# Attention, router and experts on one core: routing weights stored beside the gathered rows, a smaller index table, and a new order of loads and router work

## The chip, the core and the metric

The kernel runs on one core of a Trainium2 chip. The metric is the device time of one execution in microseconds (us), as the median of several runs. Six names recur. PE is the matrix engine (its weight loads, PEld, run beside it), DVE the vector engine, ACT the scalar engine, POOL the GpSimd engine, SP the engine that here only issues DMAs. Each engine works through its own instructions in order and waits for the others by semaphores; DMAs run on 16 DMA engines shared by all queues.

## The reference

Two stages. The first is causal attention with a window of 64 positions, for 8 batches, 8 heads, 576 positions, 64 elements a head. Its output is written as 4608 rows of 512 floats. The second sends each row to one of 8 experts:

```python
logits = x @ w_gate                       # 4608 x 8
local_gate = sigmoid(x @ w_local)
for b in range(B):
    prev_e = -1
    for s in range(S):
        fresh_e = argmax(logits[b, s])
        e = fresh_e if s == 0 or local_gate[b, s] < 0.5 else prev_e
        prev_e = e
        p = softmax(logits[b, s])
        out[b, s] = p[e] * (relu(x[b, s] @ w1[e]) @ w2[e])
```

The expert of a row is therefore carried along the sequence until a gate lets a fresh choice in. w1[e] is 512 x 1024, w2[e] is 1024 x 512, all float32.

## The kernel before

**Attention.** There are 36 units of work: 9 stretches of 512 rows (`sc`, 0 to 8), each with 4 pairs of heads (`hp`). For a unit (sc, hp), `scores` puts a product of q and k into PSUM and ACT takes the exponential (L414). Then the window's mask is applied in one of two ways. For most units DVE multiplies by a mask (L419, 128x1024). For the units listed in `BIASED` PE adds a large negative bias in bfloat16 ahead of the exponential, six more matmuls, and DVE has nothing to do. `values` multiplies by v on PE (L429) into a pair of PSUM banks, of which there are two; DVE takes the reciprocal of the row sums (L434), for sc of 4 and more the gate columns (L437), and writes x (L439), which frees the pair. Scores are two units ahead (`LEAD`). At a stretch's last unit x goes to `xs` in device memory by a DMA on POOL. `xs` holds 4608 rows of 512 floats and two rows of zeros.

**Router.** It runs twice, as a generator whose steps are laid between other work: `first` for the first T1 = 1728 rows (14 chunks of 128) while attention still runs, `second` for the other rows (23 chunks) while the first expert blocks run. `gate` finds the fresh expert and the carried one (`vk`, transposed on PE at L806; `loc` and `carry` at L816 and L826; `ex` at L838; one-hots `oh`, summed on PE) and the probability `pt` of the chosen expert. `places` gives each row a place: a slot `hi` and a row `lo` within it. `table` turns places into lists of row numbers: for each chunk, a one-hot of `lo` (`rowh`, 128 x 128, L939) times a one-hot of `hi` multiplied by five columns (`colh`, L949): the chunk number, the position in the chunk, and the probability split into three bfloat16 parts. These products are summed on PE in PSUM (L956), copied to `t` (L958) and combined to the row number `idx`, the gather list `gx`, and the probability `pw` of each slot. Ahead of the expert blocks that use the second table, a flag is transposed (L159) and read.

**Experts.** A block is a group of 256 rows (or 128, 64, 32) of one expert. Block n takes its rows with gathers on POOL (L1133, 128 rows each, in `rows`), its weights with two loads of 2 MB on SP (L1148, in `weights`, from a ring of four buffers), transposes the rows (`turn`, L1162), then `hidden` and `result`. The last multiplies by `pw` as it empties PSUM: on ACT (L1393), or on DVE (L1274), and POOL scatters y to the output. Blocks -1, -2 and -3 come from the first table, and run in a plain or half-plain way (L1356, L1388) while `second` proceeds between their matmuls; blocks from 0 on come from the second table. Most of these use a scheme with 7 products in place of 8 (L1217, L1265).

**Order.** In attention the order of PE's instructions follows a scheduler. In `run`, PE's order is that of the program (`manual_schedule`), and from block -3 on that of DVE and ACT too; SP's is not. The router's steps are laid by `step`: it is called between groups of expert matmuls, counts down a `pause` by 3.5 per call, and takes up the next router steps when `pause` is used up; each step adds its own estimated length to `pause` with `yield`. The gathers of -1 and the loads of its w1 are issued from attention, at unit (7, 1), w2 at (8, 0), each behind a small DMA (`late`) that waits for a value of that unit; blocks -2 and -3 are fetched in `run`. Gathered rows live in six buffers (`xq`; -1 has two of its own in `xp`).

Of the kernel before, what the change touches and what calls it, by code (L numbers as in the profile page):

```python
# [8 lines left out]
F32 = mybir.dt.float32  # L9
# [25 lines left out]
PIECE = 10  # L35
T1 = 3 * S
# [31 lines left out]
BIASED = [(4, 3), (5, 1), (5, 3), (6, 1), (6, 3)]  # L68
# [13 lines left out]
def kernel(  # L82
# [21 lines left out]
    xs = dram.tile([N + 2, D], F32, name="xs")  # L104
    lt = const.tile([P, C, E + 1], F32, name="lt")
    tabs = dict(idx=const.tile([P, NS], U32, name="idx"), pw=const.tile([P, NS], F32, name="pw"),
                ej=const.tile([1, NBLK + 1], I32, name="ej"), idxh=const.tile([P, E], U32, name="idxh"),
                pwh=const.tile([P, E], F32, name="pwh"),
                idxq=const.tile([P, E], U32, name="idxq"), pwq=const.tile([P, E], F32, name="pwq"), idx1=const.tile([P, FIRST], U32, name="idx1"),
                pw1=const.tile([P, FIRST], F32, name="pw1"), ej1=const.tile([1, FB], I32, name="ej1"),  # L110
# [11 lines left out]
    with ExitStack() as fast:  # L122
        ring = fast.enter_context(tc.tile_pool(name="ring", bufs=4))
        rt = Router(fast, tc, lt, tabs, ident)
        ex = Experts(fast, tc, ring, *moe)
        zrow = ex.xp.tile([P, D], F32, name="xg")[:1]
        nc.vector.memset(zrow, 0.0)
        for i in (ZR, N + 1):
            nc.gpsimd.dma_start(out=xs[i:i + 1, :], in_=zrow)
        attention(tc, ring, kq, v3, v4, vt, vh, xs, lt, ok, wgs, wg2s, ident, rt, ex)  # L130
        ex.run(fast, rt, lambda ps: flag(nc, ps, ok, bad, tabs["ej"][:, NBLK:], rare, ident))
    if_rare = nc.values_load(rare[0:1, 0:1], min_val=0, max_val=1,  # L132
                             skip_runtime_bounds_check_because="the larger of two comparisons")
    with tc.If(if_rare > 0):
        if_bad = nc.values_load(bad[0:1, 0:1], min_val=0, max_val=1,
                                skip_runtime_bounds_check_because="the result of a comparison")
        with tc.If(if_bad > 0):
            careful(tc, q, k, v, xs, lt, wgs, ident)
            with ExitStack() as slow:
                ring = slow.enter_context(tc.tile_pool(name="ring2", bufs=4))  # L140
                rt = Router(slow, tc, lt, tabs, ident)
                rt.prepare()
                ex = Experts(slow, tc, ring, *moe)
                with tc.tile_pool(name="rt_ps1", bufs=1, space=PSUM) as ps:
                    for _ in rt.first(lambda: ps.tile([P, SC], F32, name="a")):
                        pass
                ex.begin()
                ex.run(slow, rt)
# [17 lines left out]
def attention(ctx, tc, ring, kq, v3, v4, vt, vh, xs, lt, ok, wg, wg2, ident, rt, ex):  # L166
# [302 lines left out]
    for i, (sc, hp) in enumerate(units):  # L469
# [50 lines left out]
        if (sc, hp) == (NSC - 2, 1):  # L520
# [4 lines left out]
        if (sc, hp) == (NSC - 1, 0):  # L525
            ex.weights(ex.jobs[0], -1, ("w2",), lambda: until(3, allr[:1, sc, hp, 0, :1]))
        if hp == HP - 1:
# [3 lines left out]
            nc.gpsimd.dma_start(out=xs[row_of(sc * SC):row_of(sc * SC) + SC, :].rearrange("(c p) d -> p c d", p=P),  # L531
# [12 lines left out]
def careful(ctx, tc, q, k, v, xs, lt, wgs, ident):  # L544
# [107 lines left out]
    def rows(st):  # L652
# [7 lines left out]
        nc.gpsimd.dma_start(out=xs[row_of(c * P):row_of(c * P) + P, :], in_=x)  # L660
# [36 lines left out]
class Router:  # L697
# [9 lines left out]
    def __init__(self, ctx, tc, lt, tabs, ident):  # L707
        self.nc, self.lt, self.tabs, self.ident = tc.nc, lt, tabs, ident
# [7 lines left out]
    def prepare(self):  # L716
# [24 lines left out]
        self.w = tl("w", P, CV, 5, dt=BF16)  # L741
        for i, a in enumerate((0, C1)):
            c = PART[i]
            n = c.stop - c.start
            nc.vector.tensor_copy(self.w[:, a:a + n, 0], iota(f"chunk{i}", [P, n], [[1, n]], 0, c.start - C))
        nc.vector.tensor_copy(self.w[:, :, 1], iota("at", [P, CV], [[0, CV]], 1))
# [21 lines left out]
    def gate(self, part, psum):  # L768
# [109 lines left out]
        vec.tensor_tensor(pt, pt, sm, op=Alu.mult)  # L878

        w = self.w[:, cs]  # L880
        vec.tensor_copy(w[:, :, 2], pt)
        vec.tensor_tensor(pt, pt, w[:, :, 2], op=Alu.subtract)
        vec.tensor_copy(w[:, :, 3], pt)
        vec.tensor_tensor(w[:, :, 4], pt, w[:, :, 3], op=Alu.subtract)
# [43 lines left out]
    def table(self, psum, cs, ns, lo, hi, idx, pw, gx):  # L928
# [5 lines left out]
        for k in range(0, len(pieces), 2):  # L934
            built = []
            for b, m in pieces[k:k + 2]:
                rowh = self.oh_p.tile([P, PIECE, P], BF16, name="rowh")[:, :m]
                sh = [P, m, P]
                vec.tensor_tensor(rowh, self.io128.to_broadcast(sh), last(lo[:, b:b + m]).to_broadcast(sh),  # L939
                                  op=Alu.is_equal)  # L940
                yield 0.15 * m, False
                one = self.oh_p.tile([P, PIECE, 1, ns], BF16, name="one")[:, :m]
                sh = [P, m, ns]
                vec.tensor_tensor(one[:, :, 0], self.ios[:, :, :ns].to_broadcast(sh),
                                  last(hi[:, b:b + m]).to_broadcast(sh), op=Alu.is_equal)
                colh = self.oh_p.tile([P, PIECE, 5, ns], BF16, name="colh")[:, :m]
                sh = [P, m, 5, ns]
                w = self.w[:, cs.start + b:cs.start + b + m, :].rearrange("p c (k o) -> p c k o", o=1)
                vec.tensor_tensor(colh, one.to_broadcast(sh), w.to_broadcast(sh), op=Alu.mult)  # L949
                built.append((b, m, rowh, colh))  # L950
                yield 0.3 + 0.0055 * ns * m, (b, m) in (pieces[-1], pieces[k + 1:k + 2] and pieces[k + 1])
            if tab is None:
                tab = psum()[:, :5 * ns].rearrange("p (k s) -> p k s", k=5)
# [3 lines left out]
        t = self.tl("t", P, 5, NS)[:, :, :ns]  # L957
# [10 lines left out]
        vec.tensor_tensor(pw, t[:, 2], t[:, 3], op=Alu.add)  # L968
        vec.tensor_tensor(pw, pw, t[:, 4], op=Alu.add)
        return at  # L970

    def first(self, psum):
# [29 lines left out]
        yield from self.table(psum, slice(0, C1), FIRST, lo, hi, tabs["idx1"], tabs["pw1"], tabs["gx1"])  # L1002

    def second(self, psum):
# [81 lines left out]
        at = yield from self.table(psum, slice(0, CV), NS, lo, hi, tabs["idx"], tabs["pw"], tabs["gx"])  # L1086

        for i in range(2):
            vec.tensor_scalar(tabs["idxh"][i * HF:(i + 1) * HF], at[:HF, HF0:], 2.0, float(i), Alu.mult, Alu.add)
            vec.tensor_copy(tabs["pwh"][i * HF:(i + 1) * HF], tabs["pw"][:HF, HF0:])  # L1090
        a = slice(HF, HF + QR)
        for i in range(4):
            vec.tensor_scalar(tabs["idxq"][i * QR:(i + 1) * QR], at[a, HF0:], 4.0, float(i), Alu.mult, Alu.add)
            vec.tensor_copy(tabs["pwq"][i * QR:(i + 1) * QR], tabs["pw"][a, HF0:])
# [8 lines left out]
class Experts:  # L1103
# [12 lines left out]
    def rows(self, st, n):  # L1116
        tabs = self.tabs
        if n < 0:
            idx, pw, gx, rows = tabs["idx1"], tabs["pw1"], tabs["gx1"], ZR + 1
            slots = range(-2 - 2 * n, -2 * n)  # L1120
        else:
            idx, pw, gx, rows = tabs["idx"], tabs["pw"], tabs["gx"], N + 2
# [3 lines left out]
        st.update(x=[], slots=slots, idx=idx, pw=pw, rows=P, big=len(slots) == 2, fast=len(slots) == 2 and n not in PLAIN)  # L1126
# [4 lines left out]
        for s in slots:  # L1131
            x = (self.xp if n == -1 else self.xq).tile([P, D], F32, name="xg")
# [3 lines left out]
            st["x"].append(x)  # L1136
        return st
# [17 lines left out]
    def turn(self, st, quiet, later=False):  # L1155
# [3 lines left out]
        for i, x in enumerate(st["x"]):  # L1159
# [3 lines left out]
            (nc.scalar.copy if quiet else nc.vector.tensor_copy)(xt[:, :, i * P:i * P + n], tp[:, :, :n])  # L1163
        if st["fast"] and not quiet and not later:
# [84 lines left out]
    def big_result(self, st, hooks):  # L1249
# [10 lines left out]
        pw = [st["pw"][:, i:i + 1] for i in st["slots"]]  # L1260
# [38 lines left out]
    def quarter(self, st):  # L1299
# [20 lines left out]
        def two():  # L1320
# [7 lines left out]
            nc.scalar.activation(y, yp, Act.Copy, scale=self.tabs["pwq"][:, s:s + 1])  # L1328
# [36 lines left out]
    def result(self, st, step, hooks=()):  # L1365
# [3 lines left out]
        if "half" in st:  # L1369
# [8 lines left out]
            nc.scalar.activation(y[:, :w], yp[:, :w], Act.Copy, scale=self.tabs["pwh"][:, s:s + 1])  # L1378
# [6 lines left out]
        for i, s in enumerate(st["slots"]):  # L1385
# [7 lines left out]
            nc.scalar.activation(y, yp, Act.Copy, scale=st["pw"][:, s:s + 1])  # L1393
# [13 lines left out]
    def run(self, ctx, rt, last=None):  # L1407
# [4 lines left out]
        ctx.enter_context(tc.manual_schedule(engines={ET.PE}))  # L1412
# [33 lines left out]
        jobs += [self.fetch(n) for n in order[1:FB]]  # L1446
        self.turn(jobs[0], True)
        step()
        for i, n in enumerate(order):
            quiet = i < FB  # L1450
            if i == FB - 1:
# [5 lines left out]
                ctx.enter_context(tc.manual_schedule(engines={ET.PE, ET.DVE, ET.Activation}))  # L1457
# [82 lines left out]
```

## Time and profile before

| what | us |
|---|---|
| time, median of 3 runs (lowest to highest) | 653.27 (651.92 to 654.65) |
| the profiled execution's own time | 650.66 |
| its span in the profile | 648.9 |
| mean granted PE clock | 0.995 of full |
| HBM read and written | 145.85 and 19.27 MB |

The page cuts the span into 40 equal slices of 16.2 us. A digit is the busy share in tenths, 9 standing for 90% and more:

```profile
DVE  6786588954996767346371775172826663876730
ACT  3766755621111231203130223012121321123120
POOL 4422121320014110131211311021213111200001
PEclk9999998999999999999999999999999999999998
DMA  9989999796437556486966855587768655945601
```

The seven first slices are attention, with DMA nearly full. From the eighth on the expert blocks of the first table begin, with the second part of the router beside them on DVE (slices 11 to 12 show DVE full). From about the thirteenth on the blocks of the second table run to the end.

The costliest groups of the page are the experts' matmuls (L1217, L1265, L1356, L1388), 227 us of PE's 621 in their three largest rows (79.6, 77.6 and 65.9, with a fourth of 56.2 and more behind). In attention the mask is DVE's largest group: 31 multiplies of 1296 ns in the mean, 40.1 us. DMAs of 2 MB of weights take 9.1 us from issue to landing in the median, gathers of 128 rows 8.0, the scatters of y 8.1.

### The profile page before, as it was taken

How to read it: one execution, taken by the hardware profiler on the slowest of the kernel's cores; microseconds unless marked ns; L12 is line 12 of the kernel's file. 1: busy time of each engine (PE TensorE's matmuls, PEld its weight loads, DVE VectorE, ACT ScalarE, POOL GpSimd, SP SyncE). 2: the span in 40 equal slices, each digit the busy share in tenths (PEclk: the TensorE clock that was granted, in tenths of full speed). 3: DMA queues.
4: the chain of work that ended last, by engine and by line, in shares of the span. 5: the costliest groups of instructions: out<-in, count | busy, mean ns of one | idle time of the engine just before them, and what ended most of it. 6: DMA issues, size and time to landing. Idle time of an engine off the chain costs nothing. (4 is left out here: it accounts for less than half of the span.)

```text
span 648.9 us, 14685 instructions
## 1 busy us (share of the span) xinstructions
PE 620.9 (96%) x6307; PEld 535.3 (82%) x6307; DVE 402.5 (62%) x737; ACT 184.6 (28%) x323; POOL 128.7 (20%) x131
## 2 busy tenths in 40 slices
PE   8898987998999999999999999999999999999995
PEld 7777775775757999979899799978997998899994
DVE  6786588954996767346371775172826663876730
ACT  3766755621111231203130223012121321123120
POOL 4422121320014110131211311021213111200001
PEclk9999998999999999999999999999999999999998
DMA  9989999796437556486966855587768655945601
GB/s 339 410 338 376 377 369 336 267 417 261 163 144 234 190 205 250 163 289 226 388 246 225 309 185 212 220 323 287 302 212 304 246 189 181 389 166 190 236 17 39
DMA packets 22003, 165.78 MB, mean 255 GB/s; under 512 B 3457, under 2 KB 4487, under 8 KB 11944
## 3 DMA queue, kind: packets, MB, share of 16 engines
q1 hardware_dynamic: 13112, 135.24, 56.6%
q0 software_dynamic: 8816, 29.50, 11.7%
q8 instruction: 52, 0.85, 0.5%
q14 instruction: 23, 0.19, 0.1%
HBM read 145.85 MB, written 19.27 MB: 254 GB/s over the span
## 5 line engine op out<-in xcount | busy, mean ns | idle before, releaser
L1338 POOL DMA_INDIRECT out_dram<-y,idx x36 | 41.8, 1162 | 313.7 <-DVE y L1274 127.1
L1217 PE MATMUL hp<-xs,ws 128*128 128x128 f32 x672 | 79.6, 275 | 0.0
L1265 PE MATMUL hp<-ws,hs 128*128 128x256 f32 x336 | 77.6, 380 | 0.0
L1217 PEld LDWEIGHTS hp<-xs,ws 128*128 128x128 f32 x672 | 77.3, 192 | 0.0
L1265 PEld LDWEIGHTS hp<-ws,hs 128*128 128x128 f32 x336 | 63.5, 190 | 9.3 <-issue 0.8
L1356 PE MATMUL hp<-xt,w 128*64 128x64 f32 (+2 forms) x640 | 65.9, 275 | 0.0
L1274 DVE SCALAR_TENSOR_TENSOR y<-hp,pw,kept 128x256 f32<-128x256 f32 x42 | 19.7, 481 | 73.1 <-issue 44.1
L1356 PEld LDWEIGHTS hp<-xt,w 128*128 128x128 f32 (+1 forms) x640 | 60.8, 170 | 4.6 <-issue 1.1
L1133 POOL DMA_INDIRECT xg<-xs,gx x40 | 46.7, 1168 | 82.1 <-PE tp L1162 68.5
L1228 DVE TENSOR_TENSOR h<-hp,keep 128x512 f32<-128x512 f32 x42 | 28.7, 690 | 52.7 <-PE hp L1217 52.0
L1388 PE MATMUL yp<-w,h 128*128 128x512 f32 x128 | 56.2, 592 | 0.0
L1217 PEld LDWEIGHTS hp<-xt,w 128*128 128x128 f32 x448 | 53.2, 192 | 2.7 <-issue 1.3
L1217 PE MATMUL hp<-xt,w 128*128 128x128 f32 x448 | 54.7, 275 | 0.0
L1265 PE MATMUL hp<-w,h 128*128 128x256 f32 x224 | 53.6, 382 | 0.0
L429 PE MATMUL xo<-vb,p 128*64 128x74 f32 (+1 forms) x576 | 44.3, 229 | 8.9 <-DVE x L439 4.0
L419 DVE TENSOR_TENSOR p<-p,mask 128x1024 f32<-128x1024 f32 x31 | 40.1, 1296 | 16.5 <-ACT p L414 16.3
L429 PEld LDWEIGHTS xo<-vb,p 128*64 128x64 f32 x576 | 38.7, 138 | 13.8 <-issue 6.3
L414 ACT ACTIVATE p<-sp 128x512 f32<-128x512 f32 x72 | 39.1, 596 | 33.2 <-PE sp L383 31.1
L383 PEld LDWEIGHTS sp<-w 64*64 64x64 f32 x1296 | 37.5, 136 | 11.9 <-issue 8.4
L1265 PEld LDWEIGHTS hp<-w,h 128*128 128x128 f32 x224 | 41.3, 190 | 5.6 <-issue 0.4
L1388 PEld LDWEIGHTS yp<-w,h 128*128 128x128 f32 x128 | 23.7, 190 | 26.8 <-issue 25.8
L383 PE MATMUL sp<-w 64*64 64x128 f32 (+1 forms) x1296 | 42.7, 267 | 1.7 <-ACT p L414 1.1
(284 smaller groups left out, 955.4 us busy)
## 6 DMA issues: line engine op xcount, KB each, us to landing
w<-in_w_dram SPq DMA_DIRECT2D x48, 2048.0 KB, 9.1
w<-in_kq_dram SPq DMA_DIRECT2D x17, 1024.0 KB, 9.8
xs<-x POOLq DMA_DIRECT2D x9, 1024.0 KB, 12.2
va<-in_v_dram SPq DMA_DIRECT2D x5, 1184.0 KB
vtt<-in_vt_dram SPq DMA_DIRECT2D x5, 1024.0 KB, 5.9
va<-in_v_dram SPq DMA_DIRECT2D x3, 1040.0 KB, 9.2
va<-in_v_dram SPq DMA_DIRECT2D x2, 520.0 KB, 8.0
w<-in_kq_dram SPq DMA_DIRECT2D x2, 512.0 KB, 3.8
```

The lines of the kernel that those rows point to most:

```text
L383: nc.tensor.matmul(sp[j][c * WIN:(c + 1) * WIN, a:b], lhsT=kt[h, hp, block * WIN:(block + 1) * WIN], rhs=qt[h, hp, a:b], start=not biased, ...
L414: nc.scalar.activation(p[:, j], sp[j], Act.Exp, scale=DH ** -0.5)
L419: masked.append(nc.vector.tensor_tensor(p, p, m.to_broadcast([P, 2, SC]), op=Alu.mult))
L429: nc.tensor.matmul(xo[par * WIN:(par + 1) * WIN, j, s * VW:s * VW + n], lhsT=p[:, j, b * WIN:(b + 1) * WIN], rhs=w[:, s, 2 * hp + j, :n], ...
L1133: self.nc.gpsimd.indirect_dma_start(out=x, out_offset=None, in_=self.xs[:rows, :], in_offset=bass.IndirectOffsetOnAxis(ap=gx[:, s:s + 1], ...
L1217: nc.tensor.matmul(out[:, m, :], lhsT=a[:, kk, m * P:(m + 1) * P], rhs=b[:, kk, :], start=start and m + kk == 0, stop=stop and (m, kk) == ...
L1228: nc.vector.tensor_tensor(o, x, y, op=add)
L1265: nc.tensor.matmul(out, lhsT=a[:, m, :], rhs=b[:, m, :], start=start and m == 0, stop=stop and m == FK // 2 - 1, skip_group_check=True)
L1274: nc.vector.scalar_tensor_tensor(y[i][:, j * w:(j + 1) * w], x, pw[i], y2, Alu.mult, Alu.add)
L1338: self.nc.gpsimd.indirect_dma_start(out=self.out[:, :], out_offset=bass.IndirectOffsetOnAxis(ap=st["idx"][:, s:s + 1], axis=0), in_=y, in_ ...
L1356: nc.tensor.matmul(hp[a, i, :], lhsT=st["w1"][:, kk, m * P:(m + 1) * P][:, a], rhs=st["xt"][:, kk, :n], start=(kk == 0), stop=(kk == DK - 1))
L1388: nc.tensor.matmul(yp, lhsT=st["h"][:, m, i * P:(i + 1) * P], rhs=st["w2"][:, m, :], start=(m == 0), stop=(m == FK - 1))
```

## The change

- Rows of `xs` become 528 floats wide (`PITCH`). The 16 added floats hold the row's probability. `weigh` writes them from SP, with a run of 64 bytes for each row: part 0 in two DMAs for 1728 rows, part 1 in three for 2880; the added floats of a few rows between the parts are zeroed at the start from POOL. A gathered tile then has its probabilities in a column, and `result` uses that column (`st["pw"]`) in place of the table's; halves and quarters copy it to a tile of their own.
- The table has two columns (chunk and position) in place of five, made by two DVE operations of 54 columns a chunk. The matmuls of the second table are 108 wide instead of 270, those of the first 12 instead of 30. The five small operations that split the probability, and those that put it together, go.
- The second table's row one-hots are made on ACT: for each of 37 slices of 128 x 128 the absolute value of `lo` less a ramp, then four times (10 slices at a time, or what is left) one less that, cut at zero. The first table's stay on DVE.
- In `run`, SP follows the order of the program too. The gathers of -2 and -3 are issued first, and a small DMA (`held`) on SP waits for the second gather of -2 before the weights of -2 and -3 are issued.
- The gates of the loads of -1 move two units ahead: w1 from (7, 1) to (6, 3), w2 from (8, 0) to (7, 1).
- Units (6, 0) and (6, 2) become biased.
- After the first `step` in `run` the pause is 2.0 longer. In PE's order the transposes of `vk` then come behind 32 matmuls of `hidden(-1)` and not 16, and the later router steps move back likewise.

```diff
-BIASED = [(4, 3), (5, 1), (5, 3), (6, 1), (6, 3)]
+BIASED = [(4, 3), (5, 1), (5, 3), (6, 0), (6, 1), (6, 2), (6, 3)]
...
-    xs = dram.tile([N + 2, D], F32, name="xs")
+    xs = dram.tile([N + 2, PITCH], F32, name="xs")
...
+        nc.gpsimd.dma_start(out=xs[T1:ZR, D:].rearrange("(c p) o -> p c o", p=HF),
+                            in_=zeros[:HF, :n * (PITCH - D)].rearrange("p (c o) -> p c o", c=n))
...
-        if (sc, hp) == (NSC - 2, 1):
+        if (sc, hp) == (NSC - 3, 3):
             ex.jobs = [ex.weights({}, -1, ("w1",), lambda: until(2, allr[:1, sc, hp, 0, :1]))]
...
-        if (sc, hp) == (NSC - 1, 0):
+        if (sc, hp) == (NSC - 2, 1):
             ex.weights(ex.jobs[0], -1, ("w2",), lambda: until(3, allr[:1, sc, hp, 0, :1]))
...
-        vec.tensor_tensor(pt, pt, sm, op=Alu.mult)
-
-        w = self.w[:, cs]
-        vec.tensor_copy(w[:, :, 2], pt)
-        vec.tensor_tensor(pt, pt, w[:, :, 2], op=Alu.subtract)
-        vec.tensor_copy(w[:, :, 3], pt)
-        vec.tensor_tensor(w[:, :, 4], pt, w[:, :, 3], op=Alu.subtract)
+        self.pt = tl("ptw", P, CMAX, PITCH - D)[:, :n]
+        wide = [P, n, PITCH - D]
+        vec.tensor_tensor(self.pt, last(pt).to_broadcast(wide), last(sm).to_broadcast(wide), op=Alu.mult)
+
+    def weigh(self, part):
+
+        chunks, xs = PART[part], self.xs
+        c = chunks.start
+        for a, b in ((0, T1), ) if not part else ((T1, ZR), (ZR, N)):
+            for a, b in ((a, -(-a // P) * P), (-(-a // P) * P, b // P * P), (b // P * P, b)):
+                if a >= b:
+                    continue
+                i, n, p = a // P, max(1, (b - a) // P), min(P, b - a)
+                self.nc.sync.dma_start(
+                    out=xs[row_of(a):row_of(a) + b - a, D:].rearrange("(c p) o -> p c o", p=p),
+                    in_=self.pt[a % P:a % P + p, i - c:i - c + n])
...
-                vec.tensor_tensor(colh, one.to_broadcast(sh), w.to_broadcast(sh), op=Alu.mult)
+                vec.tensor_tensor(colh[:, :, 0], one, last(self.chunk[:, cs.start + b:cs.start + b + m]).to_broadcast(sh),
+                                  op=Alu.mult)
+                vec.tensor_scalar(colh[:, :, 1], one, self.at, None, Alu.mult)
                 built.append((b, m, rowh, colh))
+                if ns != FIRST:
+                    for i in range(m):
+                        nc.scalar.activation(rowh[:, i, :], self.io128[:, 0, :], Act.Abs, bias=lo[:, b + i:b + i + 1],
+                                             scale=-1.0)
+                    nc.scalar.activation(rowh, rowh, Act.Relu, bias=self.ones[:, :1], scale=-1.0)
+                yield 0.6 if ns == FIRST else 0.42 * m, (b, m) in (pieces[-1], pieces[k + 1:k + 2] and pieces[k + 1])
...
-        vec.tensor_tensor(pw, t[:, 2], t[:, 3], op=Alu.add)
-        vec.tensor_tensor(pw, pw, t[:, 4], op=Alu.add)
...
+        self.weigh(1)
+        at = yield from self.table(psum, slice(0, CV), NS, lo, hi, tabs["idx"], tabs["gx"])
...
-            x = (self.xp if n == -1 else self.xq).tile([P, D], F32, name="xg")
+            x = (self.xp if n == -1 else self.xq).tile([P, PITCH], F32, name="xg")
...
+        st["pw"] = [x[:, D:D + 1] for x in st["x"]]
...
-        ctx.enter_context(tc.manual_schedule(engines={ET.PE}))
+        ctx.enter_context(tc.manual_schedule(engines={ET.PE, ET.SP}))
...
-        jobs += [self.fetch(n) for n in order[1:FB]]
+        jobs += [self.rows({}, n) for n in order[1:FB]]
+        held = self.one.tile([1, 1], F32, name="held")
+        self.nc.sync.dma_start(out=held, in_=jobs[1]["x"][1][:1, :1])
+        for i, n in enumerate(order[1:FB]):
+            self.weights(jobs[1 + i], n)
         self.turn(jobs[0], True)
         step()
+        pause += 2.0
```

## Prediction

> **What bounds the kernel.** I read the page's busy times first, then the list of waits of PE, then windows of the stretches in which those waits lie.
>
> ```profile
> PE 620.9 (96%) x6307; PEld 535.3 (82%) x6307; DVE 402.5 (62%) x737; ACT 184.6 (28%) x323; POOL 128.7 (20%) x131
> ```
>
> PE is busy for all but 28 of 648.9 us, so the time moves only by PE's own work, by its waits, or by its clock. The waits (total us, times, longest):
>
> ```profile
> PE xo L429 <- DVE x L439: 4.0, 2, 2.7
> PE tp L1162 <- DMA xg<-xs,gx: 1.9, 1, 1.9
> PE r L159 <- DVE t L958: 1.4, 1, 1.4
> PE r L806 <- DVE vk L799: 1.2, 1, 1.2
> ```
>
> Each has one or two occurrences. The timeline puts them at 100.57 (1.36) and 105.53 (2.66), 151.13 (1.95), 200.91 (1.37) and 137.63 (1.17). After 201 us PE has no gap above 0.2 us: nothing can be won there. Windows around the first (PE, PEld, DVE, ACT, POOL, clock, DMA share, GB/s):
>
> ```profile
> 98.00:102.00 4.00, 2.64 (x84) 2.34 (x82) 3.81 (x17) 3.45 (x5) 1.06 (x2) 1.00 1.01 415
> 102.00:106.00 4.00, 1.34 (x50) 1.20 (x44) 4.00 (x8) 1.08 (x2) 0.00 (x0) 1.00 1.02 321
> 106.00:110.00 4.00, 4.00 (x63) 2.18 (x62) 3.86 (x10) 0.58 (x1) 0.00 (x0) 0.57 0.79 311
> ```
>
> From 98 to 110 DVE is full and PE idle beside it; behind the 2.66 us gap PE runs at half clock from 105.97 to 109.3 (pairs of value matmuls 0.125 us apart, not 0.063), which costs 1.65 us more.
>
> **The sum**, against the profiled execution (650.66 us; 1.8 lie around its span). It is 2.6 below the median 653.27, so I carry a difference over to the median.
>
> *Attention, 93 to 111 us.* Two masks of 1.22 us (1.13 from one start to the next) leave DVE: units (6,0) at 91.3 and (6,2) at 103.27. The built order lists also move router work: the casts, the 1280-wide row one-hot (1.49) and a small compare now stand ahead of x of (5,3), the 512-wide one and both column products ahead of x of (6,0). x(5,3): 100.5 − 1.1 − 0.3 (small weight operations merged) + 2.4 = 101.5. x(6,0): 105.47 − 2.26 − 0.3 + 1.45 = 104.4. So values of (6,1) start near 101.5 instead of 100.57, those of (6,2) near 104.4 instead of 105.53, and (6,3), 5.37 later before, follows 5.37 − 1.65 (full clock) + 0.28 later: 108.4 instead of 110.9. **Gain 2.5**. The 0.28 is what a biased unit added to PE (its spacing from a neighbour that isn't: 98.13 against 97.85 in one measured stretch); it is in the sum once here, the other one falls into the gap.
>
> The new gap ahead of (6,1) is about 2.06 (101.5 less 99.2 + 0.28, where PE ran out before). Will it halve the clock? The rows: a gap of 2.66 did, one of 1.36 did not; halfway between is 2.0. The Trainium skill ("TensorE: Matmul & The Clock Gate", *What's actually happening*) asks for an idle window of about 3.4 us, so by the rule it stays full and the gain is 2.5; but the rule would have spared the 2.66 gap too, and didn't. At half clock the gain is 0.9. I take 2.5, with PE at work before and behind, and keep 0.9 for the range.
>
> *Router wait, L806.* Transposes of vk move from behind 16 matmuls of hidden(-1) to behind 32; 16 take 3.62 us, the wait was 1.17 and goes. DVE's later chain has the next 32 matmuls. **Gain 1.17** (0.8 to 1.2).
>
> *Gather of -2, L1162.* Its gathers were issued at 135.6 and 136.9 on POOL and landed at 151, with DMA at 0.98 to 1.03 busy from 140 to 155: 8 MB of weights issued from 119.99 to 130.7 share the engines. Now SP waits (held) till these gathers are in, then issues w of -2 and -3. Queued behind that wait: four weight loads, the weigh of the second part, everything later on SP. First needed is w1 of -2, after 167: with gathers in by about 142, two loads of about 10 us are in by 162. Cover 5 us. **Gain 1.95** (1.5 to 1.95).
>
> *Table matmuls.*
>
> ```profile
> 184.75 2.50 PE L956 MATMUL r<-colh,rowh 128*128 128x270 bf16 x20
> ...
> 197.39 2.15 PE L956 MATMUL r<-colh,rowh 128*128 128x270 bf16 x17
> ```
>
> 20 starts fill 184.75 to 187.09, 0.117 us each. The first table's 14 of 30 columns take 0.45: 0.032. At 108 columns I interpolate 0.05: 37 × 0.067. **Gain 2.5** (2.0 to 2.9). The first table's saving is under 0.1.
>
> *Flag, L159.* PE waited 1.37: DVE finished a ws sum (till 200.42), then a 270-column copy of 0.43. DVE loses 5.54 of row one-hots and most of 11.0 of five-column products in 155 to 200, so the sum no longer stands in the way; a copy of 108 columns is 0.2 to 0.3, plus some 0.3 of hand-over. **Gain 0.75** (0 to 1.1). What follows, gx, comes earlier by the same.
>
> *Row one-hots on ScalarE*: the page "ScalarE: Activation LUTs", section *Rules for kernel authors*, speaks against it: Relu and the like belong on VectorE, faster in bf16. The rows: DVE 5.54 us for the whole; ScalarE's nearest is
>
> ```profile
> L1328 ACT ACTIVATE qy<-yp,pwq 128x128 f32<-128x128 f32 x2 | 0.7, 367 | 2.9 <-PE yp L1325 2.9
> ```
>
> less about 0.09 of overlap between two in a row, so 37 × 0.28 + 4 Relu (three of 1280, about 1.3, one of 0.95) = 15 us. The rule makes it a loss of 10 us. But ScalarE has nine operations from 166 to 198 (about 5.5 us) and DVE is full from 160 to 200 but for one slice; the cost is only what PE comes to wait. lo is ready some 14 us behind the matmul on oh; the 20 table matmuls stand 30 us behind it in PE's order, the 17 at 37: 22.6 us for these 15 and for the four or five operations of ScalarE between (3 us). Where the order mixes them I count 0.8 us to spare at the tightest, a Relu of hidden. Queued behind an Abs chain: Relu of hidden, copies of xt and y, each of which could be late by one batch (4 us), for which PE has two buffers. **Loss 0.5** (0 to 2).
>
> *Weights gathered with rows.* Small DVE operations go (eight copies and sums behind the table, five ahead of it; off PE's path). Rows get 2112 bytes instead of 2048, 3%: nothing, the landing of 8 us hides it. Added on SP: 1728 descriptors of 64 B ahead of the gather for -1, 2880 ahead of those for n ≥ 0; on POOL 320 at the start. No row shows one. The nearest is
>
> ```profile
> q0 software_dynamic: 8816, 29.50, 11.7%
> ```
>
> 0.117 × 16 × 648.9 / 8816 = 0.138 us a packet (of 3.3 KB). "DMA: Bandwidth & Descriptors", section *Specifications*, is the rule against: under 512 B a write to HBM becomes read-modify-write. Lower end: bytes alone, 0.138 × 64 / 3300, next to nothing. Upper: twice the row, 0.28. I take 0.1, as 64 B move less than 3.3 KB. First part: 1728 × 0.1 / 16 = 11 us; it starts when the router has its weights, near 98 to 105, behind kq and v loads, and ends by about 116 to 120. The gather (119.3 and 120.6 before) may come 3 us late; its turn is about 127 and its landing 4 to 8 us. **Loss 0.7** (0 to 3). Second part: behind w2 of -3 on the same queue (issued about 161, in by 169), so 169 + 18 = 187. The gathers want to go at about 194 (202.2 before, less the 8 gained); cover 7 us, and 3.4 more till the turn of block 0. **Nothing**; if the cover is gone, it is the slower rival.
>
> *xg held till a block's last y.* Gathers for block i+2 now wait for the last y of block i−1, not for its turn on PE: 127 us of POOL's own waits show it has room, and a block (22 us or more) lies between issue and turn against a landing of at most 15.5. Scatters stand behind gathers on POOL, but wait for the same y. **Nothing** (0 to 1 in all).
>
> *SP in program order, gates of w1 and w2 of -1 earlier by two units.* In 106 to 122 DMA is 0.46 to 0.83 busy, so 4 MB there take nobody's place. The gap of 1.55 at 128.66 has no releaser in the trace: −0 to 1.5; I take **0.3 gained**.
>
> *Start.* The added zeroing is on POOL and DVE beside the masks, on which the first mask of p waits: **loss 0.2** (0 to 0.6).
>
> Sum: 2.5 + 1.17 + 1.95 + 2.5 + 0.75 + 0.3 − 0.5 − 0.7 − 0.2 = 7.8. The profiled execution becomes 642.9; the median 653.27 − 7.8 = **645.5 us**.
>
> **Rivals.**
> 1. *The waits move, not go* (22%). Half clock after (6,1) (−1.6), gather of -1 late by 3 (−2.3), one-hots late by 2 (−1.5): 2.4 left, 650.9. For it: the gap of 2.06, and how exactly the Abs chain fits. Against: all three would have to happen; with one of them it is 647 to 648. Range 648.5 to 652.
> 2. *More than counted* (9%). No losses (+1.4), the whole 128.66 gap (+1.2), table at its low end, flag gone: 653.27 − 11.6 = 641.7.
> 3. *Slower: small descriptors* (7%). The gathers of block 0 wait for the 2880. At c us each they end at 169 + 180 c; PE waits from 194 + 3.4, so from c = 0.158. It outweighs the gain of 7.8 at c = 0.20. At 0.28 they end at 219.4, 22 us late: 653.27 − 7.8 + 22 = 667. For it: no row shows such writes and the rule makes them dear. Against: twice the cost of packets fifty times as large.
>
> **Numbers.** The main case has 62% and its range is 643 to 648.5. A measurement tells 0.5%, 3.3 us, from nothing; below 650.0 counts as faster. Faster: 0.62 + 0.09 + half of 0.22 = 0.82; same 0.11; slower 0.07. The range, from rival 2's middle to rival 1's, is 640.5 to 651.
>
> **What would show it.** PE's waits after: no L429 wait above 2.3 and a full clock from 104 to 110 (first step); no tp wait on xg for -2, no wait at the vk transposes; table matmuls 0.05 apart; a flag wait of 0.6. Against me: a tp wait for -1 near 127 or for block 0 near 206 with a DMA as releaser; a table matmul that waits for ACT's rowh; clock below 0.9 near 102; gathers later than the y they free from by more than a block.

## The result, and the profile after

The changed kernel takes 650.13 us in the median of 9 runs (647.49 to 651.83); the kernel before, beside it, 653.5 (651.92 to 655.69). The ratio is 0.9941, with a 95% interval from 0.992 to 0.9963: faster by 3.4 us, and clear of no change. 7.8 us had been forecast. The time lies within the range of the prediction, but less than half of the gain came.

The list of PE's waits after the change (total us, times, longest), to be held against the one of before:

```profile
PE xo L430 <- issue: 4.9, 4, 2.3
PE xo L430 <- DVE x L440: 2.9, 2, 2.5
...
PE sp L384 <- issue: 2.4, 4, 1.1
...
PE hp L1375 <- issue: 0.9, 3, 0.4
...
PE r L160 <- DVE t L974: 0.4, 1, 0.4
```

The waits for vk (1.2) and for the gathered rows of -2 (1.9) are gone, and the flag's fell from 1.4 to 0.4. The wait for x stands at 2.9 where 4.0 stood. On top is now something else: "issue", time for which the profile names nobody, 4.9 and 2.4 us at the two matmuls of attention, and 0.9 at L1375, which had none. The two rows of before, under the numbers that the lines had there:

```profile
PE xo L429 <- issue: 3.0, 3, 1.5
...
PE sp L383 <- issue: 0.7, 2, 0.4
```

To see where time was won and lost I took, from each trace, the start of the first values matmul of some units, of the flag's transpose and of the last matmul (us; two profiles of before and two of after, the second of each taken with the experiments, and those of some experiments). Attention runs to 132.8 us before, into the ninth of the page's 40 slices, so the first three columns lie in it:

```
                      start of (5,1)  (5,1)-(7,0)  (7,0)-(8,3)  (8,3)-flag  flag-end
before                     87.02        26.11 *      18.43        69.35      441.12
before, again              87.43        24.55        18.97        68.85      441.66
after                      89.35 *      25.25        20.08        62.31      443.18
after, again               88.29        24.60        21.93 *      62.31      443.16
gates_back                 88.10        25.61 *      19.06        62.31      443.20
gates_back_again           87.68        24.70        18.17        62.31      443.19
w2_late                    89.16        24.32        18.71        62.31      443.81
both_late                  87.72        25.68        16.98        75.09 *    443.13
gates_only                 87.84        24.52        25.61 *      67.51 *    441.66
masks_only                 87.81        24.28        20.84 *      67.61      441.70
eight_x                    87.47        25.21        17.89        62.31      442.46
nine_x                     87.62        25.70        17.85        62.31      443.54
* with a stretch of 3.4 us at half clock in it, about 1.6 us each (in both_late 13.7 us long, most of it while PE waits)
```

From the end of attention to the flag the change wins 7.0 and 6.5 us, a little more than the 6.4 that the steps there had been given. It loses on both sides of that: 1.1 to 3.5 us in the last units of attention (1.6 of the 3.5 a half clock), and 1.5 to 2.1 behind the flag, where nothing had been expected. The rows of the table matmuls and of the flag, in the timeline after:

```profile
187.75 1.13 PE L972 MATMUL r<-colh,rowh 128*128 128x108 bf16 x20
...
195.65 0.99 PE L972 MATMUL r<-colh,rowh 128*128 128x108 bf16 x17
197.00 0.27 PE L160 MATMUL r<-ident,ok 128*1 128x128 f32 x1 [0.36 <-DVE t L974]
```

20 table matmuls now fill 0.97 us (187.75 to 188.72), 0.0485 each, where 0.05 was interpolated.

Both profiles of before (650.66 and 650.76 us) lie below the lowest of its nine runs above (651.92), so profile against profile shows less gain than the medians do: 0.5 to 0.9 us (650.13 and 649.87 after) and not 3.4. What a slower execution of before loses besides was not seen.

### The profile page after: what moved, and what is told of

Its sections match the earlier page's. It is cut to its first block, busy times and chain, and to the rows that moved or that the text cites. A ratio compares the mean times of both kernels' runs of the same rounds, so it can differ in the third digit from the quotient of the medians.

```text
span 648.4 us, 14791 instructions
## 1 busy us (share of the span) xinstructions
PE 620.2 (96%) x6319; PEld 536.8 (83%) x6319; DVE 386.3 (60%) x730; ACT 199.9 (31%) x364; POOL 130.7 (20%) x132
## 5 line engine op out<-in xcount | busy, mean ns | idle before, releaser
L1375 PE MATMUL hp<-xt,w 128*64 128x64 f32 (+2 forms) x640 | 66.3, 276 | 0.9 <-issue 0.9
L1375 PEld LDWEIGHTS hp<-xt,w 128*128 128x128 f32 (+1 forms) x640 | 61.2, 170 | 5.9 <-issue 2.5
L1293 DVE SCALAR_TENSOR_TENSOR y<-hp,xg,kept 128x256 f32<-128x256 f32 x42 | 19.7, 481 | 71.4 <-issue 47.0
L1147 POOL DMA_INDIRECT xg<-xs,gx x40 | 48.7, 1217 | 44.7 <-issue 37.8
L420 DVE TENSOR_TENSOR p<-p,mask 128x1024 f32<-128x1024 f32 x29 | 35.7, 1231 | 19.9 <-ACT p L415 19.8
L430 PE MATMUL xo<-va,p 128*64 128x74 f32 (+1 forms) x576 | 44.7, 230 | 0.8 <-issue 0.8
```

Of the source, the lines that this page charges most:

```text
L420: masked.append(nc.vector.tensor_tensor(p, p, m.to_broadcast([P, 2, SC]), op=Alu.mult))
L430: nc.tensor.matmul(xo[par * WIN:(par + 1) * WIN, j, s * VW:s * VW + n], lhsT=p[:, j, b * WIN:(b + 1) * WIN], rhs=w[:, s, 2 * hp + j, :n], ...
L1147: self.nc.gpsimd.indirect_dma_start(out=x, out_offset=None, in_=self.xs[:rows, :], in_offset=bass.IndirectOffsetOnAxis(ap=gx[:, s:s + 1], ...
L1293: nc.vector.scalar_tensor_tensor(y[i][:, j * w:(j + 1) * w], x, pw[i], y2, Alu.mult, Alu.add)
L1375: nc.tensor.matmul(hp[a, i, :], lhsT=st["w1"][:, kk, m * P:(m + 1) * P][:, a], rhs=st["xt"][:, kk, :n], start=(kk == 0), stop=(kk == DK - 1))
```

## The experiments

Most kernels were timed beside the kernel before, and their ratios are to it; all left a profile. The theory that grew from the profile is A: the loads of w1 and w2 of -1, moved two units ahead, fill the DMA engines while attention still needs its PE instructions fetched. Its rival B: the unnamed gaps fall by chance.

**Where the unnamed gaps come from.** These are three of them in the timeline after, each in the middle of a unit's scores or values, where nothing new is needed:

```profile
114.12 0.44 PE L384 MATMUL sp<-w 64*64 64x128 f32 x6 [1.09 <-issue]
...
124.85 0.22 PE L430 MATMUL xo<-va,p 128*64 128x74 f32 x1 [0.80 <-issue]
...
131.58 0.22 PE L430 MATMUL xo<-vb,p 128*64 128x74 f32 x1 [2.30 <-issue]
```

The page lists a DMA queue "instruction" (packets, MB, share of the engines' time):

```profile
q8 instruction: 52, 0.85, 0.5%
```

That is 16 KB a packet. In attention these come every 4 to 7 us. Their ends beside the ends of some gaps (us, from the records of that queue):

```
kernel            packet's end  gap's end  later by
before               127.35       128.66     1.31
after                112.71       114.12     1.41
after                123.42       124.85     1.43
after                130.10       131.58     1.48
after, again         128.86       130.14     1.28
gates_back           128.14       129.66     1.52
gates_only           122.54       124.04     1.50
masks_only           126.98       128.24     1.26
```

PE goes on 1.3 to 1.5 us after a packet is in, each time in this table.

All eighteen profiles together have 159 such gaps (over 0.15 us) up to the last values of attention. Number PE's recorded instructions in order, weight loads and those of its sequencer included: 152 of the 159 gaps then stand 193 or 194 beyond a multiple of 256, and each of these ends 1.20 to 1.62 us behind the packet of the same number: the gap of before at 128.66 stands at 20 × 256 + 193, behind the 20th packet. The other seven are of 0.30 us or less. So PE waits there for a block of its instructions; what the loads do to the length of the wait is left to the experiments.

The Trainium skill ("Runtime: NRT & Kernel Launch", *Instruction fetch mechanics*) has it that the sequencer fetches blocks of 16 KiB, 256 instructions, by a DMA queue of its own, mostly hidden. Here the blocks have that size, and in the experts' part no such wait is seen. In attention it isn't hidden when the other queues fill the engines. Windows after the change (PE, PEld, DVE, ACT, POOL, clock, DMA share, GB/s):

```profile
124.00:126.00 2.00, 1.20 (x37) 1.06 (x39) 1.49 (x3) 1.35 (x4) 0.00 (x0) 1.00 0.97 409
...
128.00:130.00 2.00, 1.27 (x41) 1.12 (x38) 1.97 (x4) 0.99 (x2) 0.00 (x0) 1.00 1.20 447
130.00:132.00 2.00, 0.42 (x13) 0.42 (x14) 1.33 (x2) 0.10 (x1) 0.00 (x0) 1.00 0.79 283
```

and the first of them before the change, with no gap:

```profile
124.00:126.00 2.00, 2.00 (x71) 1.85 (x67) 1.99 (x4) 1.08 (x2) 0.81 (x1) 1.00 1.01 428
```

A full engine alone is not enough, then: a block must also fall due in that time. The gap of before comes at the next block:

```profile
128.66 0.28 PE L429 MATMUL xo<-vb,p 128*64 128x74 f32 x1 [1.55 <-issue]
```

**gates_back** puts both gates back.

```diff
-        if (sc, hp) == (NSC - 3, 3):
+        if (sc, hp) == (NSC - 2, 1):
...
-        if (sc, hp) == (NSC - 2, 1):
+        if (sc, hp) == (NSC - 1, 0):
```

> The changed kernel with the gates of the loads of w1 and w2 of block -1 back at units (7,1) and (8,0). Theory A (the gain of attention was spent again because these 4 MB now fill the DMA engines while PE's own instructions have to be fetched): PE's gaps with no releaser between 110 and 135 us shrink from 4.2 us (1.09, 0.80, 2.30) to about 1.5, the last values of attention start 2 to 2.5 us earlier, time about 648, ratio to before about 0.991. Theory B (those gaps and the half clock fall where they fall by chance, whatever the loads do): gaps of 2 to 4 us in sum again, ratio 0.994 as for the whole change.

647.0 us, ratio 0.9889 (0.9843 to 0.9936). Unnamed gaps from 108 us to the end of attention: 1.73, where the change has 4.2. As A said.

**after_again** and **gates_back_again**, side by side on one chip.

> The changed kernel unchanged, beside the others on one chip and with a second profile. Theory A (early loads of w1 and w2 of -1 make PE's instructions late): PE's gaps with no releaser from 108 us to the end of attention are 3 to 5 us in sum again; ratio to before about 0.994. Theory B (chance): the sum is anything from 1.5 to 5; same ratio.

> The changed kernel with both gates back, a second time. Theory A: gaps with no releaser of 1.5 to 2 us in sum from 108 us to the end of attention, 2.5 to 4 us faster than the changed kernel beside it, ratio to before 0.988 to 0.990. Theory B: as the changed kernel beside it, 0.994.

The change as it was: 649.87 us, 0.9929 (0.9907 to 0.9952), gaps 2.95. With the gates back: 646.2, 0.9886 (0.9851 to 0.9921), gaps 1.09. The two intervals overlap a little, but of the fifteen runs of the change one alone (647.62) is below the slowest of the six with the gates back (648.01).

**gates_only** is the other direction: before, with the earlier gates alone.

> The kernel before with one part of the change alone: the gates of w1 and w2 of -1 two units earlier, at (6,3) and (7,1). Theory A: PE's gaps with no releaser grow to 3 to 4 us in sum from 108 us to the end of attention, (7,0) to (8,3) takes 20 to 22 us against 18.4 and 19.0; 2 to 3 us slower than before, ratio 1.003 to 1.005, less what the gather of -2 gains by weights that are in earlier (up to 2 us). Theory B: ratio 1.000 or below.

657.97 us, ratio 1.0064 (1.0029 to 1.0098): slower than before by 4.2. The gaps are 3.29 in sum. Its list of waits holds a second loss, the rows of -1, which wait behind the same loads:

```profile
PE xo L429 <- issue: 4.7, 4, 1.7
...
PE tp L1162 <- DMA xg<-xs,gx: 2.0, 1, 2.0
```

Two half clock stretches lie in it too (131.8 and 138.7), and the order of SP is not the program's there, so it loses more than the same edit does beside the rest of the change.

The same two blocks of instructions can be compared in all eighteen profiles, by their number in PE's order (gaps in us):

```
                      gates of before   gates two units earlier   no load in attention
                      (11 profiles)     (6 profiles)              (both_late)
block at number 5057  no gap            five of 0.74 to 2.24      no gap
block at number 5313  0.77 to 1.89      1.70 to 2.85              no gap
```

The six are after, after_again, gates_only, two_masks_back, pause_back (the one without a gap at 5057) and no_held, which has the 2.85 and is a long execution; without it the upper end of the last row is 2.30. This is what decides for A: at the same instructions, the wait follows the place of the loads.

**w2_late** has w1's gate at (7,1) and w2's at the last unit.

> Gates back, and that of w2 of -1 moved three units further, to (8,3), the last unit. Theory A: after the 2 MB of w1 the DMA engines are free for the rest of attention, so the gap with no releaser near 128 us (1.58 with the gates back, 1.55 before the change) goes too: 1 to 1.5 us faster than with the gates back, ratio about 0.987. w2 of -1 is needed 20 us later, so nothing waits for it. Theory B: no difference from gates back.

647.59 us, 0.9892 (0.9856 to 0.9928): no better than gates_back. A gap of 1.75 at 129.07 stays, since w1 alone keeps DMA at 0.95 to 1.11 from 122 to 128 and a block falls due there. My expectation that w1 would be over by then was wrong.

**both_late** loads neither before attention ends.

> Gates back and then both moved to the last unit (8,3), so that no weights are loaded before attention ends. Theory A (loads delay PE's instructions): from unit (7,0) to (8,3) 17 to 17.8 us, with gaps with no releaser of less than 0.5 us in sum, against 18.2 to 19.1 with the gates back and 20.1 to 21.9 with the change as it was; then PE waits some 5 us for w1 and the whole is slower than with the gates back. Theory B (chance): gaps of 1 us or more as with the gates back.

657.52 us in its one run. The stage from (7,0) to (8,3) takes 16.98, the shortest of all, and from 113 us to the end of attention no unnamed gap of 0.1 us is left. PE then stands for the weights, twice as long as I had expected:

```profile
PE hp L1376 <- DMA w<-in_w_dram: 9.9, 1, 9.9
```

That is the price from the other side: without loads in attention PE starts the experts 10 us late. The stage from (7,0) to (8,3) is also nearly a sum of these 17.0 us and its unnamed gaps: 18.43 before (gap 1.55), 20.08 after (0.80 and 2.30).

**two_masks_back**, **gates_and_masks_back** and **masks_only**: the two biased units undone in the change, undone beside the gates, and alone in the kernel before.

```diff
-BIASED = [(4, 3), (5, 1), (5, 3), (6, 0), (6, 1), (6, 2), (6, 3)]
+BIASED = [(4, 3), (5, 1), (5, 3), (6, 1), (6, 3)]
```

> The changed kernel with the list of biased units of before, so units (6,0) and (6,2) multiply by the mask on DVE again. If the two masks were worth the 2.5 us of the prediction: 2 to 3 us slower than the changed kernel, ratio to before about 0.998, and waits on x near 101 to 108 us of 4 to 5 us in sum. If they were worth nothing, because PE stalls later anyway: ratio 0.994.

> Gates back and the list of biased units of before. If two masks off DVE are worth the 2.5 us of the prediction: 2 to 3 us slower than with the gates back, ratio about 0.993. If they are worth nothing: 0.989, with longer waits on x made good by shorter ones elsewhere.

> The kernel before with one part of the change alone: units (6,0) and (6,2) biased. By the prediction's step: (6,3) comes 2.5 us earlier, ratio 0.996. By what the profiles so far suggest: the wait on x is shared out between DVE and PE's own instructions and 0.4 us is gained, 1.6 more in an execution in which the half clock would have followed the 2.7 us wait: ratio 0.998 to 0.9995.

650.6 us, 0.9942 (0.9921 to 0.9964); 646.94, 0.9894 (0.9856 to 0.9931), against 0.9886 beside it; and 653.17, 0.9995 (0.9976 to 1.0014). The step is worth nothing that these runs can tell; a gain of 2.5 would be a ratio of 0.9962, outside the interval of masks_only. In masks_only the wait for x is of the same length, only at another unit; its row, and that of the second profile of before:

```profile
PE xo L429 <- DVE x L439: 3.3, 2, 2.9
```

```profile
PE xo L429 <- DVE x L439: 3.3, 3, 2.7
```

Two masks left DVE and the router's one-hots moved up into their place: (6,1) starts 2.3 us later than in that profile of before (103.29 and 100.98), (6,2) at the same time (106.00 and 105.93).

**pause_back** and **no_held**.

```diff
-        pause += 2.0
```

> The changed kernel without the longer pause after the first router step, so the transposes of vk stand behind 16 matmuls of hidden(-1) again. If the move is worth what was predicted: a wait at the vk transposes of about 1.2 us is back, time 1 us up, ratio 0.996; the row one-hots on ACT come one group earlier and no wait on them. If the wait is hidden or moves: ratio 0.994.

> The changed kernel without the small DMA that holds the weights of -2 and -3 back until a gather has landed. If it is worth what was predicted: the gather of -2 lands late again and PE waits about 2 us at the transposes of its rows, ratio 0.997. If DMA is free enough without it: no such wait, ratio 0.994.

pause_back: 650.34, 0.9931 (0.9906 to 0.9955). Its profile has the vk wait of 1.17 back, and one of 0.78 for ACT's h behind the one-hots; (8,3) to the flag takes 64.69, 2.4 more. The ratio doesn't show it. no_held, without the small DMA: 649.5, 0.9924 (0.9903 to 0.9944). No wait at the rows of -2, but 2.4 at those of -1. Its profiled execution took 656.88, far from the median, so I read no more from it. By the ratio holding the weights back is worth nothing here, so that the wait at the rows of -2 went away may be owed to the order of the issues alone; these runs don't separate the two.

**rows_on_dve** makes the second table's row one-hots on DVE, with gates back, and gives `yield` a shorter length for that step.

```diff
-                if ns == FIRST:
-                    sh = [P, m, P]
+                sh = [P, m, P]
...
-                    for i in range(m):
-                        nc.scalar.activation(rowh[:, i, :], self.io128[:, 0, :], Act.Abs, bias=lo[:, b + i:b + i + 1],
```

> Gates back, and the row one-hots of the second table made on DVE as before the change; PE's order is the same. If ScalarE's free time is what the change gains by: DVE is full from 160 to 200 us again and PE waits for the table or for ws, at the flag 0.4 becomes 0.9 to 1.4, ratio 0.990 to 0.991. If DVE had room once the five columns were gone: the stretch from the end of attention to the flag is 62.3 us as with ScalarE, ratio 0.989.

645.89 us, 0.9885 (0.9855 to 0.9916); (8,3) to the flag 62.31, to a hundredth what it is with ScalarE. Two windows of gates_back, then the same two of rows_on_dve; the third and fourth pairs are DVE and ACT:

```profile
170.00:180.00 10.00, 10.00 (x50) 8.49 (x49) 5.31 (x16) 8.83 (x23) 0.00 (x0) 1.00 0.57 132
180.00:190.00 10.00, 10.00 (x42) 4.88 (x42) 7.83 (x10) 5.99 (x18) 1.06 (x1) 1.00 0.53 215
```

```profile
170.00:180.00 10.00, 10.00 (x51) 8.66 (x50) 8.72 (x20) 2.29 (x5) 0.00 (x0) 1.00 0.61 149
180.00:190.00 10.00, 10.00 (x42) 4.93 (x41) 9.38 (x12) 1.15 (x2) 1.10 (x1) 1.00 0.57 224
```

In these 20 us ACT has 11.4 less to do, DVE 5.0 more, and PE is full in both: once the table had two columns, DVE had room.

**eight_x** and **nine_x**: more buffers for gathered rows. From flag to end the kernels with the change and six buffers take 443.0 to 443.2 us (443.8 once). Matmul by matmul against the first profile of before, 1.66 us of it arise in the first half block. Before:

```profile
550.19 3.95 PE L1356 MATMUL hp<-xt,w 128*64 128x64 f32 x128
```

After:

```profile
546.37 1.79 PE L1375 MATMUL hp<-xt,w 128*64 128x64 f32 x53
548.37 0.40 PE L1375 MATMUL hp<-xt,w 128*64 128x64 f32 x6 [0.21 <-issue]
549.12 0.40 PE L1375 MATMUL hp<-xt,w 128*64 128x64 f32 x6 [0.36 <-issue]
```

and POOL at that time:

```profile
546.90 0.98 POOL L1147 DMA_INDIRECT xg<-xs,gx  x1 [0.30 <-issue]
548.18 0.95 POOL L1147 DMA_INDIRECT xg<-xs,gx  x1 [0.31 <-issue]
```

Two gathers that waited for the last y of an older block are issued just here; before the change they had gone earlier.

```diff
-        self.xq = ctx.enter_context(tc.tile_pool(name="ex_xq", bufs=6))
+        self.xq = ctx.enter_context(tc.tile_pool(name="ex_xq", bufs=8))
```

> Gates back, and eight buffers for gathered rows instead of six, so that a gather need not wait for the last y of an older block. From the flag to PE's end all kernels with the change take 443.2 us, the kernel before 441.1; 1.7 of this is lost in the first half block, where a gather that was held back is issued beside its 64x64 matmuls. Theory C (the held-back gather does it): the stretch takes 441.2 to 441.5 us, ratio about 0.986 against 0.989 with six. Theory D (something else of the change, as the wider rows or the copy of their last column): 443.2 again, ratio as with six.

> Gates back, nine buffers for gathered rows (eight left one of two gathers in the first half block and 0.4 of its 1.7 us). Theory C: with no gather issued beside the 64x64 matmuls of that half block its 128 matmuls take 3.7 us as before the change, and 1.3 to 1.7 us go from the stretch from the flag to the end against six buffers; ratio 0.986 to 0.988. If a gather still falls beside them: 0.36 us per gather as with eight.

With eight, one gather is left there and 0.4 us of the 1.66, and the stretch takes 442.46, not 441.2 to 441.5; with nine none, and the 128 matmuls are whole again:

```profile
544.87 3.95 PE L1375 MATMUL hp<-xt,w 128*64 128x64 f32 x128
```

So this loss comes and goes with the gathers issued beside these matmuls. What happens between POOL's gather and PE's narrow matmuls, no view shows. The times: 645.56 us, 0.9895 (0.9871 to 0.9919), and 647.41, 0.9906 (0.9868 to 0.9943), no better than gates_back: with nine, seven gathers stand in a row at the flag, and DVE's first h of the first fast block, which comes at 200.45 in gates_back_again, comes at 204.94, with 1.4 us of waits on PE:

```profile
204.84 0.49 PE L1236 MATMUL hp<-xt,ws 128*128 128x128 f32 x2 [0.44 <-issue]
206.28 2.05 PE L1236 MATMUL hp<-xs,w 128*128 128x128 f32 x16 [0.95 <-DVE h L1247]
```

Why DVE is late there stays open.

**weigh_twice** issues the 1728 small writes a second time.

```diff
         self.weigh(0)
+        self.weigh(0)
```

> Gates back, and the 1728 writes of 64 bytes of the first part issued twice. If they are dear (DMA engines held, PE's instructions late): the gap with no releaser near 112 us (0.16 to 1.09 so far) grows by 1 us or more, or the gather of -1 comes so late that PE waits at its rows. If they are cheap: neither, and the SP queue is only 4.5 us longer at it.

646.39 us in one run. The gap near 112 us is 0.43, SP issues for 9.3 us instead of some 4.7, and the gather of -1, which here waits for the writes to land, leaves at 122.59 where it left at 118.02 and 120.00 with one write (gates_back_again and gates_back), without a wait on PE. The writes are cheap.

**before_again** is the second profile of before, in the table above.

> The kernel before, unchanged, for a second profile. Theory A: from (7,0) to (8,3) 18 to 19 us, a gap with no releaser of 1 to 2 us at w2 of -1; the half clock behind the wait on x near 105 us again, since that wait is 2.7 us long; from the flag to the end 441.1. Theory B (chance): any of these off by 1 us or more.

The wait on x is 2.65 again, but the clock stays full. Five profiles have that wait of 2.65 or 2.66, with the masks on DVE (before, before_again, two_masks_back, gates_and_masks_back, gates_only); the half clock comes at it in three.

## Why the prediction was wrong

*Gates of w1 and w2, costed at nothing, with 0.3 gained.* This is the step that failed. I read a mean DMA share of 0.46 to 0.83 from 106 to 122 us, before the loads were moved there, and concluded that 4 MB take nobody's place. But the loads, issued at 115.88 and 121.21, landed at 126.52 and 133.62, and with them the share was 0.97 to 1.20 in most of that time. What they displace moves 16 KB and is no data: PE's instructions. Two blocks came late, by 0.80 and 2.30 us (0.74 and 2.03 in the second profile, with a half clock of 1.6 behind it), where one had been late by 1.55 (1.62). The gap of 1.09 at 114 us is older than these loads; it is 0.16 to 0.71 in other profiles and part of what chance does. Undoing the gates gains 0.43% beside the change (0.9929 and 0.9886, 2.8 us; 3.7 by the medians of the two, 649.87 and 646.2); alone they cost 4.2. The gap at 128.66 was in the prediction, with no releaser and "0.3 gained"; it was the sign, and it grew to 2.30.

*Two masks off DVE, costed at 2.5 gained.* Mis-sized: 0.3 alone by the ratio, within noise. (6,2) did come 0.9 us earlier against (5,1), as worked out (1.1). But 1.65 of the 2.5 was the half clock, counted as if every execution of before had it, and with the change (6,3) then follows 3.8 to 5.4 us later instead of 4.0 (7.6 in the long execution of no_held), since late instruction blocks can fall between (0.2 to 1.3 us near 106 to 108 in seven profiles). Its own sign failed too: the wait ahead of (6,1), worked out at 2.06 and to stay below 2.3, was 2.52 in the first profile after, with a full clock.

*xg held until the last y, costed at nothing, up to 1.* The room that I checked was that of the landing, and there it was right. The cost lies where the gather is issued: 1.66 us at the first half block. Another 0.26 at the second half block stays with nine buffers, where no gather stands beside it; its cause is open.

*Router wait, gather of -2, table, flag.* Predicted 1.17 + 1.95 + 2.5 + 0.75 = 6.4, measured 7.0 and 6.5 in that stretch; the flag's wait went to 0.36, not 0.6. By the ratios, pause and held each show nothing when undone, so the stretch is sure as a whole, its shares from the profile only.

*ScalarE's one-hots, loss 0.5; gather of -1, loss 0.7.* Neither was seen: no wait for rowh, none for the rows of -1. The rule that such work belongs on VectorE would have made it a loss of 10; it made no difference of either sign.

*Small writes, rival 3.* 0.1 us a descriptor was taken, 0.138 the row and 0.28 the dear end. The 2880 land between 174.06 and 178.02, 0.022 us a packet on each of 16 engines. That rival is out by a factor of nine. The gather of block 0 waits for DVE's gx and nobody else:

```profile
198.44 0.99 POOL L1147 DMA_INDIRECT xg<-xs,gx  x1 [0.64 <-DVE gx L983]
```

*The rivals.* 650.13 lies in the range of rival 1, and near the upper end of the whole range, but by luck: none of its three causes came. The clock was full behind (6,1), and PE waited neither for the rows of -1 nor for the one-hots. (The whole range begins at 640.5, while the middle of rival 2, which it names, is 641.7.)

*Start.* Up to (5,1) the kernels with the change and no half clock take 87.1 to 89.2 us; before and its two variants 87.0 to 87.8. The small zeroing was given 0.2. Most of the spread is again unnamed gaps (1.2 to 4.0 us up to 90 in the one group, 2.2 to 5.3 in the other); whether the change has part in it stays open.

Added up, 7.8 − 3.1 (gates, 0.3 gained against 2.8 lost) − 2.2 (masks) − 2.0 (behind the flag) + 0.4 (the stretch to the flag, mean of two) + 1.2 (losses that didn't come) gives 2.1, against 3.4 by the medians. No kernel tried is clearly better than the change with its gates back: 0.9889 and 0.9886, some 7.3 us faster than before. That this is near the 7.8 forecast is luck, for the masks and the gathers are still wrong in it. The profiles of gates_back and gates_back_again are only 3.6 and 4.7 us faster than the faster one of before; the rest of the gain by medians lies in executions of which there is no profile, and stays open.

## What to carry to other kernels

A mean DMA share below one, read before a load is moved there, doesn't tell who will wait for a place once it is: look in the waits for gaps with no releaser, and in the records of the instruction queue for blocks that fall due in that time. Here the part with many short matmuls needed a block every 4 to 7 us and suffered; behind attention, where blocks came 9 to 35 us apart until the last 20 us, no such gap was seen. And a stall that follows another by chance, like a half clock, enters a sum with its share of the executions, not as a whole.

## What had not been expected of the hardware

- When PE waits for its next block of instructions, it resumes 1.2 to 1.6 us after the packet with them has ended (152 gaps). With the loads of the change at 0.97 to 1.2 of the DMA engines this left PE idle for 0.7 to 2.3 us at a time.
- A half clock stretch was 3.41 us long (106.01 to 109.42 before, 85.47 to 88.89 after), or twice or four times that (6.83 in gates_and_masks_back, 13.65 in both_late; those at the very end of the kernels are left aside). In the first profile after the change it came behind gaps of 0.56 and 0.93 us, and not behind one of 2.52:

```profile
84.00:86.00 2.00, 1.02 (x18) 0.89 (x18) 1.70 (x6) 1.89 (x4) 1.22 (x2) 0.87 0.89 356
86.00:88.00 2.00, 2.00 (x35) 1.64 (x37) 1.49 (x6) 0.95 (x1) 0.00 (x0) 0.50 0.93 317
```

- Writes of 64 bytes to device memory ran at 0.011 us a packet in the median, 0.022 from one to the next on an engine.
- The 128 narrow matmuls (64 x 64) of the first half block took 0.4 us longer beside one gather issued on POOL and 1.7 beside two. The first packet of the gathers' data came at 550.15 in the first profile after, when PE's gaps were over. Gathers beside 128x128 matmuls (521.70, 523.69 and 537.33 there) left no gap.
